# Seven-product matmuls one block earlier, sums kept in PSUM, and two units of work moved up

## The chip, the cores and the metric

The kernel runs on one core of one Trainium2 chip. The metric is device time in microseconds (us), the median of several runs. The engines are TensorE (PE in the rows; PEld is its weight load), VectorE (DVE), ScalarE (ACT), GpSimd (POOL) and SyncE (SP), which here issues most of the transfers. Each engine executes its own list of instructions in order and waits on semaphores for the others.

## The reference

Three parts follow one another: an attention with a memory term (B = 4, H = 8, S = 576, D = 64, so 2304 tokens), a first feed-forward layer (512 → 2048 → 512, softplus) and a second (512 → 2048 → 512, squared relu).

```python
local = softmax(causal(q @ k.T / 8)) @ v
mem = (phi(q) @ M_prev) / (phi(q) @ z_prev + 1e-06)
x = g * mem + (1 - g) * local          # 2304 tokens x 512
h = x @ w_in;  x = softplus(h) @ w_out    # layer 1
h = x @ w_in;  y = relu(h) ** 2 @ w_out   # layer 2, other weights
```

## The kernel before

Numbers are kept as a high and a low 16-bit part, so each product of two matrices is three matmuls on TensorE (high·high, high·low, low·high). The weights come as 64-bit data in 32 pieces per layer (512 KB each, buffer `wst`) and are converted on VectorE (L480 to L482, L490) and ScalarE (L489).

**Attention and layer 1.** Attention runs over 18 chunks of 128 tokens, in steps of a chunk and a group of heads: scores into `s_ps` (L342), the mask and the exponential, a transposing DMA (`PT`), the product with V into `pvt` (L399, L390). Layer 1 works on blocks of 256 tokens, `kb` = 0 to 8 there, and is cut into units: `h` (24 matmuls into `hps`, L502 to L504, then four ScalarE operations and two on VectorE that end in `g`, L506 to L513), `x` (96 matmuls into `xps`, L519 to L521), `xq` (a quarter of the contraction of block 0, into `xacc`, L564 to L566) and `w` (conversion of one piece). The units stand in a queue and are put between the attention steps as long as their added time stays under a limit; the limit for the queue ahead of a block leaves `LEAD_NS` (15000) of it for behind the last step. While layer 1's weights are still coming, block 0 is worked in quarters, and part of the units of block 1 is mixed in.

**Layer 2.** The weights W3 and W4 take memory that the attention used, and their conversion begins when it is free. The first 512 tokens are done plainly: `plain_h` (matmuls of 512 columns, L793 to L795, relu L797, square L798, a high part by a cast on VectorE, L801, and a low part, L802), then four `row_tile` (L988 to L990). The other seven blocks of 256 tokens (`kb` = 2 to 8 from here on) go by a scheme of seven products in place of eight: `x_parts`, `sums_w3` and `sums_w4` build sums of the inputs and of the weights (`XT`, `WS`, `WT`), `seven_h` does the first product of a block in two halves (q = 0, 1; each 7 × 24 matmuls of 128 columns), `parts` splits its result into `GA` and sums `GS`, and `seven_o` does the second product (two calls, together 168 matmuls of 256 columns). `plain_o` does the second product without the scheme (96 matmuls of 512 columns, L975 to L977); block 2 (`NPL` = 1) and block 8 use it. In both schemes each product has a PSUM bank of its own (pool `mm2`, eight banks), and VectorE adds it to the results (L886 to L895, L944).

A list scheduler orders each engine's instructions from the order of the code and priorities.

Of the kernel before, what the change touches and what calls it, by code (L numbers as in the profile page):

```python
# [8 lines left out]
F32 = mybir.dt.float32  # L9
# [9 lines left out]

LAG = 4  # L20
LEAD_NS = 15000.0
FR = 0.4
W1R = 1
B1Q = 3
# [19 lines left out]
NST = 3  # L44
PTB = 4
PB = 2
NPL = 1
W4A = (0, 2)
W4B = {1: (4,), 2: (6,)}
P16 = 2  # L50
ST2 = 4
DL = 2
# [3 lines left out]
def kernel(  # L56
# [101 lines left out]
    zc = att.tile([P, 2, B * H], F16, name="zc")  # L158

    def z_setup():  # L160
        zr = stage.tile([B * H, 2, D], F32, name="zr", bufs=1)
# [328 lines left out]
        dve.tensor_tensor(lo, u, hi, ALU.subtract)  # L490

    g_t = {}

    def unit_h(kb, fp):
# [15 lines left out]
        g = [w1p.tile([P, 2, NB], F16, name=f"g{t}_{fp}") for t in range(2)]  # L510
# [65 lines left out]

    load("k", 0)
    load("q", 0)
    load("k", 1, stage)
    load("v", 0)  # L580
    gates()
    z_setup()
# [113 lines left out]
    for kb in range(1, NBLK + 1):  # L696
        if kb == 1:
            lim = FR * sum(unit_time(u) for u in queue)
        else:
            lim = sum(unit_time(u) for u in queue) - LEAD_NS  # L700
        end = ready_step(kb) if kb < NBLK else s - 1
        if kb < NBLK:
            tot_c = sum(step_cost(i) for i in range(s, end + 1))
# [13 lines left out]
        if kb == 1:  # L717
            done = 4 - sum(u[0] == "xq" for u in queue)
            if done < 4:
                at = 0  # L720
                while done < B1Q:
                    done += queue[at][0] == "xq"
                    at += 1
                nh = 2 * done
                early = new[:nh] + [("x", kb, c, 0, 2 * nh) for c in range(NCC // 2)]
                out_q = queue[:at]
                for u in queue[at:]:
                    if u[0] != "w" and early:
                        out_q += early
                        early = []  # L730
                    out_q.append(u)
                    if u[0] == "w" and early:
                        out_q.append(early.pop(0))
                queue = out_q + early + [("close",)]
                if done < 4:
                    new = new[nh:]
                    xs = [("x", kb, c, 2 * nh, NFC) for c in range(NCC // 2)]
            else:
                queue.append(("close",))
# [13 lines left out]
    def w34_to(m):  # L753
        nonlocal nxt
        while nxt < m:
# [2 lines left out]
                pieces[nxt + ST2] = load_piece(nxt + ST2, (moe2_w_in, moe2_w_out), sp, st2)  # L758
            nxt += 1

    for n_, u in enumerate(queue):
        run_unit(u)
        w34_to(NPC * (n_ + 1) // nu)
    mm_cm.__exit__(None, None, None)
    pv_cm.__exit__(None, None, None)
    sps_cm.__exit__(None, None, None)
# [5 lines left out]
    mm2 = ctx.enter_context(tc.tile_pool(name="mm2", bufs=8, space=PSUM, reuse_waits="tile"))  # L772
    u2 = S_R / S_X2
    SO = 1.0 / (S_R * S_R)
    HF = NFC // 2
# [5 lines left out]


    def plain_h(j):
        x = x_t[0]
        new_g(j)
        for h in range(2):
            for i in range(2):
                f = h * HF + j + i
                ps = mm2.tile([P, 512], F32, tag="mm2", name="h2ps")
                for c in range(NCC):  # L790
                    wh, wl = (w[:, c, f * P:(f + 1) * P] for w in W3)
                    xh, xl = (x[:, t * NCC + c] for t in range(2))
                    pe.matmul(ps, wh, xh, start=(c == 0), stop=False)  # L793
                    pe.matmul(ps, wh, xl, start=False, stop=False)
                    pe.matmul(ps, wl, xh, start=False, stop=(c == NCC - 1))  # L795
                r = bp.tile([P, 512], F32, name="r2", bufs=3)
                act.activation(r, ps, AF.Relu, scale=u2)  # L797
                act.activation(r, r, AF.Square)  # L798
                hi, lo = (g[:, h, :, i * 256:(i + 1) * 256] for g in gg[j])
                r = r.rearrange("p (a t) -> p a t", a=2)  # L800
                dve.tensor_copy(hi, r)  # L801
                dve.tensor_tensor(lo, r, hi, ALU.subtract)  # L802


# [63 lines left out]
    def seven_h(kb, q):  # L868
        X = XT[kb % 2]

        def prod(w, x):
            ps = mm2.tile([P, 512], F32, tag="mm2", name="h2ps")
            for i in range(4):
                o = ps[:, i * P:(i + 1) * P]
                for k in range(2):
                    wh, wl = w3_at(w, k, 4 * q + i)
                    xh, xl = (y[:, x, k * P:(k + 1) * P] for y in X)
                    pe.matmul(o, wh, xh, start=(k == 0), stop=False)  # L878
                    pe.matmul(o, wh, xl, start=False, stop=False)  # L879
                    pe.matmul(o, wl, xh, start=False, stop=(k == 1))  # L880
            return ps.rearrange("p (j t) -> p j t", j=4)
# [12 lines left out]
        dve.tensor_tensor(r11, prod(1, 1), r11, ALU.add)  # L894
        dve.tensor_tensor(r12, prod(5, 2), r12, ALU.add)  # L895
        act.activation(r[0], r[0], AF.Relu, scale=u2)
        act.activation(r[0], r[0], AF.Square)

# [24 lines left out]
            sp.dma_start(out=out[p0:p0 + k_, :].rearrange("p (a c) -> p a c", a=2), in_=o[r0:r0 + k_])  # L923

    OB = {}


    PR = {1: (0, 0), 2: (1, 1), 4: (2, 5), 6: (3, 6), 7: (4, 4), 3: (5, 2), 5: (6, 3)}

    def seven_o(kb, which):  # L930
        def prod(n):
            gi, wi = PR[n]
            ps = mm2.tile([P, 512], F32, tag="mm2", name="ops")[:, :256]
            for j in range(HF):
                g = GA[kb, j // 4][:, :, gi] if gi < 3 else GS[kb, j // 4][:, :, gi - 3]
                gh, gl = g[:, 0, j % 4], g[:, 1, j % 4]
                wh, wl = w4_at(wi, j)
                pe.matmul(ps, gh, wh, start=(j == 0), stop=False)  # L938
                pe.matmul(ps, gh, wl, start=False, stop=False)  # L939
                pe.matmul(ps, gl, wh, start=False, stop=(j == HF - 1))  # L940
            return ps

        def add(o, ps, y):
            dve.scalar_tensor_tensor(o, ps, SO, y, ALU.mult, ALU.add)  # L944

        if which == 0:
            OB[kb] = TS[:, :, NB:]
        o = OB[kb]
        o11, o12, o21, o22 = (o[:, i] for i in range(4))
        if which == 0:  # L950
            act.activation(o12, prod(6), AF.Copy, scale=SO)
            add(o21, prod(7), o12)
            p5 = prod(5)
            add(o22, p5, o21)
            add(o12, p5, o12)
            add(o12, prod(3), o12)
            return
        p1 = prod(1)
        act.activation(o11, p1, AF.Copy, scale=SO)
        add(o[:, 1:], p1.rearrange("p (a c) -> p a c", a=1).to_broadcast([P, 3, 256]), o[:, 1:])  # L960
        add(o11, prod(2), o11)
# [35 lines left out]
    for j in range(0, HF, 2):  # L997
        plain_h(j)
        w34_to(NPC + 2 * j + 4)
    st2_cm.__exit__(None, None, None)  # L1000
    sp2 = ctx.enter_context(tc.tile_pool(name="sums", bufs=1, reuse_waits="tile"))
    WS = [sp2.tile([P, 4, 2, DFF // 2], t, name=f"WS{i}") for i, t in enumerate((F16, BF16))]
# [24 lines left out]
    for kb in range(K0, NBLK):  # L1027
        plain = kb < K0 + NPL or kb == NBLK - 1
        if K0 < kb < NBLK - 1:
            x_parts(kb + 1)  # L1030
        seven_h(kb, 0)
        if K0 < kb <= K0 + NPL:
            plain_o(kb - 1)
        elif kb > K0:
# [38 lines left out]
```

## Time and profile before

| | us |
|---|---|
| median of 3 runs | 943.59 (941.1 to 945.34) |
| profiled execution, its own time | 943.42 |
| its span | 941.6 |
| TensorE busy | 880.2 (93%) |
| VectorE busy | 728.3 (77%) |
| ScalarE busy | 613.6 (65%) |

The span runs from the first to the last recorded work of that execution; 1.8 us lie around it. Busy is time with an instruction in work on the engine. A busy TensorE isn't TensorE at its peak: its granted clock stands beside it in the rows. "X <- Y" among waits means that the first was ready to go but for the second.

### The profile page before, as it was taken

How to read it: one execution, taken by the hardware profiler on the slowest of the kernel's cores; microseconds unless marked ns; L12 is line 12 of the kernel's file. 1: busy time of each engine (PE TensorE's matmuls, PEld its weight loads, DVE VectorE, ACT ScalarE, POOL GpSimd, SP SyncE). 2: the span in 40 equal slices, each digit the busy share in tenths (PEclk: the TensorE clock that was granted, in tenths of full speed). 3: DMA queues.
4: the chain of work that ended last, by engine and by line, in shares of the span. 5: the costliest groups of instructions: out<-in, count | busy, mean ns of one | idle time of the engine just before them, and what ended most of it. 6: DMA issues, size and time to landing. Idle time of an engine off the chain costs nothing.

```text
span 941.6 us, 24682 instructions
## 1 busy us (share of the span) xinstructions
PE 880.2 (93%) x10385; PEld 730.7 (78%) x10394; DVE 728.3 (77%) x1474; ACT 613.6 (65%) x1160; POOL 2.2 (0%) x10
## 2 busy tenths in 40 slices
PE   5757999889999898999999999999999999999997
PEld 3346888679878897899988887444776999999983
DVE  6798999878757676667856699999997998767640
ACT  7977688679769695867958375663266656444530
POOL 0000000000000000000000000000000000000000
PEclk9879899899999999999999999999999999999999
DMA  9999998799876978658845666500000000000001
GB/s 234 205 217 203 223 206 177 133 150 150 130 131 117 144 134 127 116 101 131 136 86 75 171 199 182 178 22 23 24 2 24 2 24 1 25 24 2 24 13 34
DMA packets 285023, 101.24 MB, mean 108 GB/s; under 512 B 248048, under 2 KB 284400, under 8 KB 284912
## 3 DMA queue, kind: packets, MB, share of 16 engines
q1 hardware_dynamic: 284672, 99.65, 53.3%
q8 instruction: 81, 1.33, 0.6%
q14 instruction: 30, 0.25, 0.1%
q10 hardware_dynamic: 240, 0.02, 0.0%
HBM read 48.78 MB, written 4.72 MB: 57 GB/s over the span
## 4 chain that ended last, share of the span: by engine, by line
PE 52%; DVE 22%; ACT 10%; DMA 10%; issue 5%; SPq 0%; ACTq 0%; DVEq 0%
PE h2ps L878 4%; PE h2ps L879 4%; PE h2ps L880 4%; PE hps L503 4%; PE hps L502 4%; DMA rawq<-in_q_dram 4%; PE hps L504 4%; DMA PT<-p 3%; PE ops L940 3%; PE ops L938 3%; PE ops L939 3%; DVE wcv L481 3%; PE s_ps L342 3%; PE xps L520 3%; PE xps L519 3%
## 5 line engine op out<-in xcount | busy, mean ns | idle before, releaser
L502 PE MATMUL hps<-x,W 128*128 128x256 f16 x576 | 157.5, 275 | 3.8 <-DVE spa L509 1.8
L503 PE MATMUL hps<-x,W 128*128 128x256 f16 x576 | 158.1, 275 | 0.5 <-ACT x L545 0.4
L504 PE MATMUL hps<-x,W 128*128 128x256 f16 x576 | 157.8, 275 | 0.0
L520 PE MATMUL xps<-g,W 128*128 128x256 f16 x512 | 138.8, 273 | 2.4 <-DVE g L513 2.4
L519 PE MATMUL xps<-g,W 128*128 128x256 f16 x512 | 137.8, 273 | 3.3 <-ACT g L512 3.3
L521 PE MATMUL xps<-g,W 128*128 128x256 f16 x512 | 138.8, 273 | 0.0
L351 ACT ACTIVATE Pt<-Pt,cs 128x128 f32<-128x128 f32 (+4 forms) x144 | 84.6, 588 | 45.1 <-DVE cs L347 45.0
L342 PE MATMUL s_ps<-KT,qT 128*128 128x128 f16 (+2 forms) x992 | 75.4, 219 | 22.1 <-DVE cs L347 20.8
L375 DVE TENSOR_TENSOR p<-Pt,p 128x512 f16<-128x512 f32 (+2 forms) x100 | 66.5, 665 | 30.0 <-ACT p L374 29.8
L342 PEld LDWEIGHTS <-qT 128*128 128x128 f16 (+1 forms) x992 | 56.2, 103 | 40.3 <-issue 32.6
L347 DVE CUSTOM_DVE_ANT_0 Pt<-s_ps,mask 128x128 f32<-128x128 f32 (+3 forms) x128 | 61.8, 483 | 19.5 <-PE s_ps L342 19.2
L374 ACT ACTIVATE p<-Pt 128x512 f16<-128x512 f32 (+2 forms) x100 | 60.5, 605 | 15.0 <-DMA PT<-p 14.1
L503 PEld LDWEIGHTS <-W 128*128 128x128 f16 x576 | 56.8, 99 | 9.6 <-issue 3.4
L502 PEld LDWEIGHTS <-W 128*128 128x128 f16 x576 | 56.9, 99 | 7.7 <-DVE spa L509 1.1
L504 PEld LDWEIGHTS <-W 128*128 128x128 bf16 x576 | 56.8, 99 | 7.2 <-issue 0.8
L399 PE MATMUL pvt<-V,PT 128*128 128x64 f16 (+1 forms) x1392 | 58.8, 196 | 1.3 <-DMA PT<-p 1.3
L513 DVE TENSOR_TENSOR g<-spa,g 128x512 f16<-128x512 f32 x72 | 49.4, 685 | 11.2 <-ACT g L512 11.0
L509 DVE SCALAR_TENSOR_TENSOR spa<-hps,spa 128x512 f32<-128x512 f32 x72 | 49.4, 686 | 9.5 <-ACT spa L508 9.2
L519 PEld LDWEIGHTS <-W 128*128 128x128 f16 x512 | 50.0, 98 | 8.7 <-issue 3.3
L521 PEld LDWEIGHTS <-W 128*128 128x128 bf16 x512 | 50.1, 98 | 8.1 <-issue 2.7
L399 PEld LDWEIGHTS <-PT 128*128 128x128 f16 (+1 forms) x1392 | 51.2, 103 | 6.1 <-issue 2.1
L520 PEld LDWEIGHTS <-W 128*128 128x128 f16 x512 | 50.1, 98 | 5.2
(248 smaller groups left out, 2564.8 us busy)
## 6 DMA issues: line engine op xcount, KB each, us to landing
wst<-in_moe_w_in_dram SPq DMA_DIRECT2D x32, 512.0 KB, 4.7
wst<-in_moe_w_out_dram SPq DMA_DIRECT2D x32, 512.0 KB, 4.6
rawk<-in_k_dram SPq DMA_DIRECT2D x16, 256.0 KB, 4.2
rawq<-in_q_dram SPq DMA_DIRECT2D x16, 256.0 KB, 4.3
rawv<-in_v_dram SPq DMA_DIRECT2D x16, 256.0 KB, 3.4
out_dram<-T SPq DMA_DIRECT2D x12, 256.0 KB, 2.4
PT<-p SPq DMA_TRANSPOSE x100, 3.5
mraw<-in_M_prev_dram SPq DMA_DIRECT2D x8, 128.0 KB, 4.5
```

The source lines that it names most:

```text
L342: pe.matmul(o[x * n:(x + 1) * n], qT[g][:, t * H + h, x * n:(x + 1) * n], KT[kb][:, h, a - j * P:e - j * P], start=(t == 0), stop=(t == 1),)
L347: dve.tensor_tensor_reduce(out=pw, in0=view, in1=mw, scale=-0.125, scalar=3.0e38, op0=ALU.add, op1=ALU.min, accum_out=cs[:, 0, h:h + 1],)
L351: act.activation(pf, pf, AF.Exp, bias=cs[:, 0, h:h + 1], scale=-1.0, accum_out=cs[:, 1, h:h + 1],)
L374: act.activation(v16[:, :, 0], p, AF.Copy)
L375: p_lo.append(dve.tensor_tensor(v16[:, :, 1], p, v16[:, :, 0], ALU.subtract).ins.name)
L399: m = pe.matmul(o[r], t[:, o0 + i + y, r], V[kb][:, z, h, :], start=(i == 0 and y + z == 0), stop=(i == nb - 1 and y > 0),)
L502: pe.matmul(o, wh, x[:, c], start=(c == 0), stop=False)
L503: pe.matmul(o, wh, x[:, NCC + c], start=False, stop=False)
L504: pe.matmul(o, wl, x[:, c], start=False, stop=(c == NCC - 1))
L519: pe.matmul(ps, wh, gh, start=(f == f0), stop=False)
L520: pe.matmul(ps, wh, gl, start=False, stop=False)
L521: pe.matmul(ps, wl, gh, start=False, stop=(f == f1 - 1))
```

## The change

1. `NPL` becomes 0: block 2's second product too is done by `seven_o`; its `parts` build all sums, and the sums of W4 are made one step earlier (`W4B`).
2. In `seven_h` and `seven_o` one bank now takes four products (a), one two (c), one a single one (b). On the way a ScalarE copy takes partial results out between two products of the bank. Adds on VectorE per half of `seven_h` go from seven to three, per block of `seven_o` from six to three.
3. The last two `h` units of block 1 stand in the queue ahead of the last `xq`.
4. The limit ahead of the last block leaves 30000 in place of 15000.
5. The first two of the 16 products of `plain_h` are done into the two banks of `s_ps`, ahead of the last block's `x` units; `mm2` has six banks until `plain_h` ends, then a pool of eight follows.
6. `plain_h`'s high part is a ScalarE copy.
7. `seven_h(2, 0)` stands ahead of the last `row_tile`; the small tile `zr` and the second load of k use other buffers.

```diff
-NPL = 1
+NPL = 0
-W4B = {1: (4,), 2: (6,)}
+W4B = {0: (4,), 1: (6,)}
...
-            lim = sum(unit_time(u) for u in queue) - LEAD_NS
+            lim = sum(unit_time(u) for u in queue) - (LEAD_LAST if kb == NBLK - 1 else LEAD_NS)
...
+                at = queue.index(("xq", 0, 3))
+                queue[at:at] = new[nh:]
                 if done < 4:
-                    new = new[nh:]
+                    new = []
...
+    def h2_mm(ps, f):
+        x = x_t[0]
+        for c in range(NCC):
+            wh, wl = (w[:, c, f * P:(f + 1) * P] for w in W3)
+            xh, xl = (x[:, t * NCC + c] for t in range(2))
+            pe.matmul(ps, wh, xh, start=(c == 0), stop=False)
+            pe.matmul(ps, wh, xl, start=False, stop=False)
+            pe.matmul(ps, wl, xh, start=False, stop=(c == NCC - 1))
+
     for n_, u in enumerate(queue):
+        if n_ == nu - NCC // 2:
+            for f in range(2):
+                h2_mm(s_ps[:, f], f)
         run_unit(u)
...
-                dve.tensor_copy(hi, r)
+                act.activation(hi, r, AF.Copy)
                 dve.tensor_tensor(lo, r, hi, ALU.subtract)
...
-        act.activation(r11, prod(0, 0), AF.Copy)
-        dve.tensor_tensor(r12, prod(3, 4), r11, ALU.add)
-        dve.tensor_tensor(r22, prod(4, 5), r12, ALU.add)
-        dve.tensor_tensor(r21, prod(2, 6), r22, ALU.add)
-        p5 = prod(6, 3)
-        dve.tensor_tensor(r22, p5, r22, ALU.add)
-        dve.tensor_tensor(r12, p5, r12, ALU.add)
-        act.activation(r[1], r[1], AF.Relu, scale=u2)
+        (a, a4), (b, b4), (c, c4) = bank(), bank(), bank()
+        prod(a, 0, 0, True, True)
+        act.activation(r11, a4, AF.Copy)
+        prod(c, 6, 3, True, True)
+        prod(a, 3, 4, False, True)
+        act.activation(r12, a4, AF.Copy)
+        prod(b, 1, 1, True, True)
+        dve.tensor_tensor(r11, b4, r11, ALU.add)
+        prod(a, 4, 5, False, True)
+        act.activation(r22, a4, AF.Copy)
+        dve.tensor_tensor(r22, c4, r22, ALU.add)
+        prod(a, 2, 6, False, True)
+        act.activation(r21, a4, AF.Relu, scale=u2)
+        act.activation(r22, r22, AF.Relu, scale=u2)
         act.activation(r[1], r[1], AF.Square)
-        dve.tensor_tensor(r11, prod(1, 1), r11, ALU.add)
-        dve.tensor_tensor(r12, prod(5, 2), r12, ALU.add)
+        prod(c, 5, 2, False, True)
+        dve.tensor_tensor(r12, c4, r12, ALU.add)
...
         if which == 0:
             OB[kb] = TS[:, :, NB:]
+            AC[kb] = bank(), bank()
...
+            prod(a, 1, True)
+            copy(o11, a)
+            prod(c, 5, True)
+            prod(a, 6, False)
+            copy(o12, a)
+            b = bank()
+            prod(b, 2, True)
+            add(o11, b)
+            prod(a, 7, False)
+            copy(o22, a)
+            add(o22, c)
+            return
+        prod(c, 3, False)
+        add(o12, c)
         store(2 * kb, o[:, :2])
-        add(o21, prod(4), o21)
+        prod(a, 4, False)
+        copy(o21, a)
         store(2 * kb + 1, o[:, 2:])
...
-    for m in range(XB // P):
+    for m in range(XB // P - 1):
         row_tile(0, m, XB // 2)
+    seven_h(K0, 0)
+    row_tile(0, XB // P - 1, XB // 2)
```

How instructions stand on the engines, at three places. Names carry numbers that differ between the two programs; W_70 and W_71 are layer 1's second weights there, and lines are moved by one to thirty-five.

The first is TensorE's list in the weights' stretch, before: between attention matmuls (`pvt`, `s_ps`) stand those of the last `xq` (`xacc`), and the 48 matmuls of the last two `h` units of block 1 come some hundred matmuls further on.

```order
L390 LDWEIGHTS phiT
L390 MATMUL pvt<-Mt,phiT 128x64
L390 LDWEIGHTS phiT
L390 MATMUL pvt<-Mt,phiT 128x64
L564 LDWEIGHTS W_70
L564 MATMUL xacc_982<-g_6_2588,W_70 128x256
L565 LDWEIGHTS W_70
L565 MATMUL xacc_982<-g_6_2589,W_70 128x256
L342 LDWEIGHTS qT
L342 MATMUL s_ps<-KT,qT 128x128
```

The same place after the change, some rows ahead of the first `xacc` of the last `xq`:

```order
L303 MATMUL nps<-zc,phiT 128x1
L504 LDWEIGHTS W_68
L504 MATMUL hps<-x_61,W_68 128x256
L505 LDWEIGHTS W_68
L505 MATMUL hps<-x_61,W_68 128x256
L506 LDWEIGHTS W_69
L506 MATMUL hps<-x_61,W_69 128x256
```

The `h` unit's matmuls (`hps`) now come ahead of that `xacc`, and none are left behind it until block 2's.

The second place is the end of layer 1 on TensorE, where the last `h` unit of the last block ends; before:

```order
L504 LDWEIGHTS W_69
L504 MATMUL hps<-x_2724,W_69 128x256
L519 LDWEIGHTS W_70
L519 MATMUL xps<-g_0_9166,W_70 128x256
L520 LDWEIGHTS W_70
L520 MATMUL xps<-g_0_9167,W_70 128x256
L521 LDWEIGHTS W_71
L521 MATMUL xps<-g_0_9166,W_71 128x256
```

And after:

```order
L506 LDWEIGHTS W_69
L506 MATMUL hps<-x_2917,W_69 128x256
L772 LDWEIGHTS W_8815
L772 MATMUL s_ps<-x_61,W_8815 128x512
L773 LDWEIGHTS W_8815
L773 MATMUL s_ps<-x_61,W_8815 128x512
L774 LDWEIGHTS W_8816
L774 MATMUL s_ps<-x_61,W_8816 128x512
```

The `x` units' matmuls (`xps`) followed directly; now 24 matmuls of layer 2 into `s_ps`, of 512 columns, stand between.

The third is ScalarE's list at the second half of `seven_h` of block 2 (`r_...` are its results, `W_...` those of the next half or block in memory of W3); before:

```order
L885 ACTIVATE r_10469<-h2ps 128x512
L849 ACTIVATE XT_10159<-x_2722 128x256
L885 ACTIVATE W_9015<-h2ps 128x512
L822 ACTIVATE WT_10156<-T 128x2x512 x2
L892 ACTIVATE r_10470<-r_10470 128x1024
L893 ACTIVATE r_10470<-r_10470 128x1024
L892 ACTIVATE W_9016<-W_9016 128x2x512
L901 ACTIVATE GA<-r_10470 128x1024
L893 ACTIVATE W_9016<-W_9016 128x2x512
L896 ACTIVATE r_10469<-r_10469 128x1024
```

And after, where L905, L908, L912 and L915 take results out of one bank:

```order
L905 ACTIVATE r_10653<-h2ps 128x512
L864 ACTIVATE XT_10161<-x_2915 128x256
L908 ACTIVATE r_10653<-h2ps 128x512
L837 ACTIVATE WT_10158<-T 128x2x512
L912 ACTIVATE r_10654<-h2ps 128x512
L925 ACTIVATE GS<-W_8815 128x1024
L915 ACTIVATE r_10654<-h2ps 128x512
L925 ACTIVATE GS<-W_8816 128x1024
L916 ACTIVATE r_10654<-r_10654 128x512
L917 ACTIVATE r_10654<-r_10654 128x1024
```

One operation on `h2ps` per half has become four, each with other work between. On TensorE the third copy's product and its follower in that bank stand so; behind L895 of one product (weights `WS`) the next begins (weights `W`), with nothing in between:

```order
L894 LDWEIGHTS WS_10156
L894 MATMUL h2ps<-XT_10162,WS_10156 128x128
L895 LDWEIGHTS WS_10157
L895 MATMUL h2ps<-XT_10161,WS_10157 128x128
L893 LDWEIGHTS W_8815
L893 MATMUL h2ps<-XT_10161,W_8815 128x128
L894 LDWEIGHTS W_8815
L894 MATMUL h2ps<-XT_10162,W_8815 128x128
```

It is the only such place without other matmuls between two products of one bank.

## Rows read from the trace of the kernel before

**Rows 1.** The page: busy time of each engine (PE alone); granted clock in 40 slices.
```profile
PE 880.2 (93%) x10385; PEld 730.7 (78%) x10394; DVE 728.3 (77%) x1474; ACT 613.6 (65%) x1160; POOL 2.2 (0%) x10
...
PEclk9879899899999999999999999999999999999999
```

**Rows 2.** Busy time by stretch: start:end, length, engines, granted clock, DMA share, GB/s.
```profile
0.00:100.00 100.00, 67.95 (x658) 47.36 (x659) 81.12 (x221) 80.33 (x189) 2.24 (x10) 0.86 1.03 216
100.00:200.00 100.00, 88.23 (x1071) 78.11 (x1067) 89.92 (x201) 76.77 (x160) 0.00 (x0) 0.96 0.94 182
200.00:540.00 340.00, 331.38 (x4492) 294.88 (x4491) 233.22 (x528) 254.15 (x533) 0.00 (x0) 1.00 0.73 124
540.00:640.00 100.00, 98.10 (x660) 64.33 (x659) 99.05 (x186) 61.78 (x107) 0.00 (x0) 1.00 0.46 140
640.00:740.00 100.00, 97.91 (x1074) 70.22 (x1079) 91.80 (x137) 48.73 (x61) 0.00 (x0) 1.00 0.05 17
740.00:860.00 120.00, 120.00 (x1594) 113.45 (x1592) 100.25 (x158) 65.45 (x82) 0.00 (x0) 1.00 0.05 15
```

**Rows 3.** Busy time in shorter stretches, columns as above.
```profile
160.00:180.00 20.00, 16.23 (x181) 13.58 (x180) 18.33 (x41) 13.77 (x30) 0.00 (x0) 0.86 0.87 149
174.00:180.00 6.00, 5.18 (x47) 4.09 (x48) 6.00 (x13) 4.19 (x9) 0.00 (x0) 0.52 0.51 68
180.00:200.00 20.00, 15.99 (x213) 13.86 (x211) 14.42 (x34) 15.32 (x32) 0.00 (x0) 0.93 0.88 152
198.00:200.00 2.00, 2.00 (x11) 1.43 (x10) 1.52 (x4) 2.00 (x5) 0.00 (x0) 0.53 1.02 192
680.00:700.00 20.00, 18.23 (x327) 18.05 (x325) 19.89 (x32) 11.06 (x15) 0.00 (x0) 1.00 0.01 2
```

**Rows 4.** Waits of PE from 160 to 202 us: total, times, longest.
```profile
PE xps L519 <- ACT g L512: 2.5, 1, 2.5
PE xacc L564 <- ACT W L489: 2.2, 1, 2.2
```

**Rows 5.** Line L795, every third matmul of plain_h: ns, first and last start.
```profile
L795 PE MATMUL h2ps<-x,W x64: 379/379/379, 587.8 to 628.5; 128*128 128x512 f16 x64
```

**Rows 6.** Timeline of PE: 33 matmuls of 256 columns, then 40 of 128.
```profile
564.20 0.27 PE L519 MATMUL xps<-g,W 128*128 128x256 f16 x1
...
567.80 0.27 PE L519 MATMUL xps<-g,W 128*128 128x256 f16 x1
...
745.01 0.22 PE L878 MATMUL h2ps<-XT,W 128*128 128x128 f16 x1
...
747.25 0.22 PE L879 MATMUL h2ps<-XT,WS 128*128 128x128 f16 x1
```

**Rows 7.** Timeline of DVE: first conversion of W3, sixth sum of W4.
```profile
533.35 0.43 DVE L480 TENSOR_SCALAR wcv<-wst 128x512 int32<-128x512 int32 x1 [5.82 <-DMA wst<-in_moe_w_in_dram]
...
705.00 1.21 DVE L823 TENSOR_TENSOR WT<-T,WT 128x1024 bf16<-128x1024 f32 x1
```

**Rows 8.** Timeline of ACT: the last copy ahead of the last store.
```profile
936.82 0.60 ACT L978 ACTIVATE T<-ops 128x512 f32<-128x512 f32 x1 [9.12 <-PE ops L977]
```

**Rows 9.** Waits of PE from 540 to 600 us.
```profile
PE xps L520 <- DVE g L513: 1.4, 1, 1.4
PE xps L519 <- ACT g L512: 0.5, 1, 0.5
```

**Rows 10.** Waits of PE from 640 to 720 us.
```profile
PE h2ps L878 <- ACT W L897: 1.8, 1, 1.8
```

**Rows 11.** Four lines: ns least, median, most; the last with its mean.
```profile
L886 DVE TENSOR_TENSOR W<-h2ps,W x7: 679/683/684, 673.7 to 882.2; 128x512 f32<-128x512 f32 x7
...
L885 ACT ACTIVATE W<-h2ps x7: 575/597/597, 671.7 to 880.3; 128x512 f32<-128x512 f32 x7
...
L801 DVE CAST gg<-r x16: 416/420/421, 593.0 to 632.2; 128x512 f16<-128x512 f32 x16
...
L901 ACT ACTIVATE GS<-r 128x1024 f16<-128x1024 f32 x8 | 8.4, 1050 | 8.8 <-DVE r L915 8.5
```

More of the change, by code (lines that the diff above doesn't have):

```diff
@@ L21 @@
 LEAD_NS = 15000.0
+LEAD_LAST = 30000.0
 FR = 0.4
@@ L160, in z_setup @@
     def z_setup():
-        zr = stage.tile([B * H, 2, D], F32, name="zr", bufs=1)
+        zr = att.tile([P, H, D], F32, tag="xf", name="zr")[:B * H, :2]
         z16 = stage.tile([B * H, 2, 2, D], F16, name="z16", bufs=1)
@@ L492 @@
     g_t = {}
+    hcount = [0]
     def unit_h(kb, fp):
@@ L509, in unit_h @@
         dve.scalar_tensor_tensor(a, ps, 0.0, a, ALU.max, ALU.add)
-        g = [w1p.tile([P, 2, NB], F16, name=f"g{t}_{fp}") for t in range(2)]
+        slot = hcount[0] % (NFC // 2)
+        hcount[0] += 1
+        g = [w1p.tile([P, 2, NB], F16, name=f"g{t}_{slot}") for t in range(2)]
         g_t[kb, fp] = g
@@ L578 @@
     load("q", 0)
-    load("k", 1, stage)
+    load("k", 1)
     load("v", 0)
@@ L765 @@
     pv_cm.__exit__(None, None, None)
-    sps_cm.__exit__(None, None, None)
     w1_cm.__exit__(None, None, None)
@@ L771 @@
     bp = bp_cm.__enter__()
-    mm2 = ctx.enter_context(tc.tile_pool(name="mm2", bufs=8, space=PSUM, reuse_waits="tile"))
+    mm2_cm = tc.tile_pool(name="mm2", bufs=6, space=PSUM, reuse_waits="tile")
+    mm2 = mm2_cm.__enter__()
     u2 = S_R / S_X2
@@ L783, in plain_h @@
     def plain_h(j):
-        x = x_t[0]
         new_g(j)
@@ L788, in plain_h @@
                 f = h * HF + j + i
[L789 to L795, printed above, removed]
+                if f < 2:
+                    ps = s_ps[:, f]
+                else:
+                    ps = mm2.tile([P, 512], F32, tag="mm2", name="h2ps")
+                    h2_mm(ps, f)
                 r = bp.tile([P, 512], F32, name="r2", bufs=3)
@@ L869, in seven_h, with prod @@
         X = XT[kb % 2]
-        def prod(w, x):
-            ps = mm2.tile([P, 512], F32, tag="mm2", name="h2ps")
+        def prod(ps, w, x, first, last):
             for i in range(4):
@@ L877, in prod, with bank @@
                     xh, xl = (y[:, x, k * P:(k + 1) * P] for y in X)
[L878 to L881, printed above, removed]
+                    s = first and i == 0 and k == 0
+                    pe.matmul(o, wh, xh, start=s, stop=False, skip_group_check=True)
+                    pe.matmul(o, wh, xl, start=False, stop=False, skip_group_check=True)
+                    pe.matmul(o, wl, xh, start=False, stop=last and i == 3 and k == 1, skip_group_check=True)
+        def bank():
+            ps = mm2.tile([P, 512], F32, tag="mm2", name="h2ps")
+            return ps, ps.rearrange("p (j t) -> p j t", j=4)
         r = RB[2 * q:2 * q + 2]
         r11, r12, r21, r22 = r[0][:, 0], r[0][:, 1], r[1][:, 0], r[1][:, 1]
-        act.activation(r11, prod(0, 0), AF.Copy)
-        dve.tensor_tensor(r12, prod(3, 4), r11, ALU.add)
-        dve.tensor_tensor(r22, prod(4, 5), r12, ALU.add)
-        dve.tensor_tensor(r21, prod(2, 6), r22, ALU.add)
-        p5 = prod(6, 3)
-        dve.tensor_tensor(r22, p5, r22, ALU.add)
-        dve.tensor_tensor(r12, p5, r12, ALU.add)
-        act.activation(r[1], r[1], AF.Relu, scale=u2)
+        (a, a4), (b, b4), (c, c4) = bank(), bank(), bank()
[12 more added lines that the diff above has]
+        act.activation(r22, r22, AF.Relu, scale=u2)
         act.activation(r[1], r[1], AF.Square)
-        dve.tensor_tensor(r11, prod(1, 1), r11, ALU.add)
-        dve.tensor_tensor(r12, prod(5, 2), r12, ALU.add)
+        prod(c, 5, 2, False, True)
+        dve.tensor_tensor(r12, c4, r12, ALU.add)
         act.activation(r[0], r[0], AF.Relu, scale=u2)
@@ L925, with prod @@
     OB = {}
+    AC = {}
     PR = {1: (0, 0), 2: (1, 1), 4: (2, 5), 6: (3, 6), 7: (4, 4), 3: (5, 2), 5: (6, 3)}
     def seven_o(kb, which):
-        def prod(n):
+        def prod(ps, n, first):
             gi, wi = PR[n]
-            ps = mm2.tile([P, 512], F32, tag="mm2", name="ops")[:, :256]
             for j in range(HF):
@@ L937, in prod, with bank, copy, add @@
                 wh, wl = w4_at(wi, j)
[L938 to L944, printed above, removed]
+                pe.matmul(ps, gh, wh, start=(first and j == 0), stop=False, skip_group_check=True)
+                pe.matmul(ps, gh, wl, start=False, stop=False, skip_group_check=True)
+                pe.matmul(ps, gl, wh, start=False, stop=(j == HF - 1), skip_group_check=True)
+        def bank():
+            return mm2.tile([P, 512], F32, tag="mm2", name="ops")[:, :256]
+        def copy(o, ps):
+            act.activation(o, ps, AF.Copy, scale=SO)
+        def add(o, ps):
+            dve.scalar_tensor_tensor(o, ps, SO, o, ALU.mult, ALU.add)
         if which == 0:
             OB[kb] = TS[:, :, NB:]
+            AC[kb] = bank(), bank()
+        a, c = AC[kb]
         o = OB[kb]
@@ L950, in seven_o @@
         if which == 0:
[L951 to L956, printed above, removed]
+            prod(a, 1, True)
[9 more added lines that the diff above has]
+            add(o22, c)
             return
[L958 to L961, printed above, removed]
+        prod(c, 3, False)
+        add(o12, c)
         store(2 * kb, o[:, :2])
-        add(o21, prod(4), o21)
+        prod(a, 4, False)
+        copy(o21, a)
         store(2 * kb + 1, o[:, 2:])
@@ L999 @@
         w34_to(NPC + 2 * j + 4)
+    mm2_cm.__exit__(None, None, None)
+    sps_cm.__exit__(None, None, None)
+    mm2 = ctx.enter_context(tc.tile_pool(name="mm3", bufs=8, space=PSUM, reuse_waits="tile"))
     st2_cm.__exit__(None, None, None)
@@ L1030 @@
             x_parts(kb + 1)
-        seven_h(kb, 0)
+        if kb > K0:
+            seven_h(kb, 0)
         if K0 < kb <= K0 + NPL:
```

## Prediction

> **What bounds the kernel now.** I read the page's first two parts, then busy time by stretch, then what TensorE waited for in each stretch. The reader sees in [rows 1] that TensorE is busy 880.2 of 941.6 us and that its granted clock is at nine tenths or more from the ninth slice on. By stretch [rows 2]: TensorE is idle 32.0 us in the first 100 us, where the DMA engines are full (share 1.03), 11.8 us in the next 100, 8.6 in the 340 us up to 540, and then 1.9, 2.1 and 0.0. So from 200 us on, time falls mainly where matmul time falls, and only waits that the edits touch can be added. VectorE is the second limit: 99.05 of 100 us in 540 to 640, 91.8 in the next 100. ScalarE has room everywhere (61.8, 48.7, and 65.5 of 120).
>
> Inside the second 100 us there is more to gain than idle time. From 174 to 180 the granted clock is 0.52, the 1.2 GHz level, and again 0.53 at 198 to 200 [rows 3]; the full level is 2.4 GHz. Both stretches follow waits of TensorE: 2.2 us for a converted weight ahead of xacc and 2.5 us for g ahead of xps [rows 4].
>
> **The change, part by part.**
>
> Second product of block 2: 96 matmuls of 512 columns go, 168 of 256 come. One of 512 takes (628.5 − 587.8)/189 = 0.2153 us, since the row [rows 5] is every third of 192. One of 256 takes (567.80 − 564.20)/33 = 0.109 us [rows 6]. So 20.7 us go and 18.3 come: **−2.4 us**, all on TensorE. What could take it back is that its sums of W4 and of the activations are now wanted a block, about 37 us, earlier. VectorE works without a gap from the first conversion of W3 at 533.35 us to the sixth sum of W4, which ends at 706.2 [rows 7]. Those 172.9 us hold operations whose durations add up to 188.8 us, so one follows another at 0.916 of its duration. After the change, with the new adds in and the sixteen casts and the adds of seven_h out, the same count gives 174 us to the last sum of W4, 164 us to the activation sums GS of the block's first half, and 182 to those of the second. The first conversion waits for a transfer that waits for the end of the attention (its memory is used again), so it comes at 526 to 533 us; the two GS are then ready at 690 to 697 and 708 to 715. Counted back from the last copy at 936.82 [rows 8] with these pitches and 0.056 for 128 columns (2.24 us for 40 [rows 6]), TensorE comes to them with 238 and 221 us of matmuls left, that is at about 692 and 709 if it ends 7 us earlier. It is even within a few microseconds: I take 0, with bounds 0 and +5.
>
> The waits around the end of layer 1: 24 matmuls of 512 columns (24 × 0.2153 = 5.2 us) now stand between the last h unit and the x units that waited 1.4 + 0.5 us for its g [rows 9]. Their weights are converted and their data are there, since the two pieces of W3 that they take are converted first, by 540 us, and the layer's first block is long done. 5.2 us cover 1.9: **−1.9 us**.
>
> The wait of 1.8 us in 640 to 720 for a square of seven_h(2,0) [rows 10], with VectorE busy 19.89 of 20 us there [rows 3]: four of seven VectorE adds of each half leave (8 × 0.683 = 5.5 us [rows 11]), but the fuller split of block 2 brings four of about that length and larger pieces. I take **−1.2 us**, bounds −1.8 and 0.
>
> The early units: two h units of block 1, 48 matmuls or 5.2 us at full clock, move ahead of the last xq, where TensorE waited 2.2 and then ran at half speed. The 5.2 busy us from 174 to 180 lost half to the clock, 2.6, and the 2.0 at 198 to 200 lost 1.0; with the 4.7 us of the two waits up to 8 us could come back. But VectorE is busy 18.33 of 20 us in 160 to 180 [rows 3], and each h unit gives it two operations and ScalarE four, which delays the attention's own chain. I take a third: **−3.0 us**, bounds 0 and −8. The pieces of W are converted in the same order, and the move of one DMA of k on SP's queue is in a stretch where the DMA engines are full either way: 0.
>
> The copies moved to ScalarE in plain_h: 16 × 0.42 leave VectorE [rows 11] and 16 of about 0.6 (0.597 for a copy of the same size [rows 11]) come to ScalarE, which has 38 us free in that 100. Cost 0 there; without that room it would be 10 us.
>
> Accumulation in PSUM: in each half of seven_h four products share one bank, and a ScalarE copy (0.597 us) stands between two of them; seven_o has three such places per pair. ScalarE gains about 1.35 us a half and 0.75 a seven_o, 3.5 us per block of 37, and VectorE loses 7.3 (8 × 0.683, and 1.8 of seven_o's adds). Before, every product had its own bank and TensorE is busy 120.00 of the 120 us from 740 on [rows 2]. After, the order shows what stands between two products to one bank: of some 80 places one has nothing (seven_h(2,1), the last rows of the order shown), which costs about 0.6 + 0.3 = 0.9 us; the others have 1.6 us of other matmuls or more, half of them over 2.8. A copy fits into 1.6 us unless an operation of 1.05 us [rows 11] stands ahead of it on ScalarE, which then makes it late by about 0.1. I take **+1.3 us**, bounds +0.9 and +10: the last if a fourth of the places, the tightest 20, lose 0.5 each.
>
> The Trainium skill speaks against this edit: "Perfetto Trace Analysis", section "Optimizing Tensor Performance", wants independent groups of matmuls to rotate through PSUM banks so that one's evacuation runs under the next one's matmuls. The trace of before agrees with what that buys (the same 120.00 of 120 us). By the rule the change would end at the upper bound, +10, and the time at 945.6.
>
> Attention before the last block ends 37 matmuls, 4.0 us, earlier. As much cover is gone from a stretch with 8.6 us of idle time in 340: **+0.7**, bounds 0 and +4. seven_h(2,0) before the last row_tile only fills: 0. The second product of the last block keeps its form and has about 10 us of matmuls ahead of its last input, so the end of the span (last matmul, a ScalarE copy, a store) stays.
>
> Sum: −2.4 − 1.9 − 1.2 − 3.0 + 1.3 + 0.7 = −6.5. The profiled execution took 943.42 us (span 941.6 and 1.8 around it), 0.2 under the median of 943.59, so 943.42 − 6.5 = **936.9 us**.
>
> **The rivals.**
>
> A. *The early part gives nothing.* VectorE or the transfers set the pace up to 200 us, and the h units only change places with other waits. For it: VectorE at 18.33 of 20, the DMA share. Against it: TensorE is idle 7.8 us in the 40 us from 160 on [rows 3]. Without the −3.0 the time is 939.9.
>
> B. *The sums are late.* VectorE ends its chain 5 us after TensorE wants it, and the −2.4 and −1.9 turn into waits for GS or WT at 690 to 715. For it: VectorE at 99%. Against it: 6.7 us of casts and 5.5 of adds leave this stretch. Then 936.9 + 5 = 941.9.
>
> C. *Slower: the shared bank.* ScalarE executes in order; behind an operation that waits for VectorE the copy is late, and TensorE, in order as well, stands at the next product of the bank. There are about 80 places; from 0.1 us at each on average (8 us instead of 1.3) the other gains are gone. At 0.2 us each (16 instead of 1.3) the time is 951.6; with the 10 of the bound it is 945.6. For it: three times as many handovers between ScalarE and TensorE. Against it: 1.6 us of cover, and ScalarE at two thirds.
>
> D. *The whole bound of the early part comes back.* The clock stays at full level from 172 to 202: −8 for −3, 931.9.
>
> By the Trainium skill's "Perfetto Trace Analysis", section "Matmul Optimizations", matmuls that run back to back keep TensorE's speed up, which agrees with the clock of 0.52 after the wait and would speak for D.
>
> **How the numbers follow.** The forecast (934 to 938.8) has 0.38, A 0.20, B 0.18, C 0.11 and D 0.13. A measurement of this kernel tells about 0.5% (4.7 us) from no change: under 938.9 is faster, over 948.3 slower. Faster: forecast and D, 0.51, and a third of A, where the other terms come out a little better: 0.58. Same: the rest of A, B, and a third of C: 0.35. Slower: the rest of C, 0.07. The range takes in D below, with 2 us for its own error, and leaves out the far part of C above: 930 to 946.
>
> **What would show it.** Seven-product matmuls at 256 columns in place of 512 around 700 us, and no row of a wait there over 1 us; else B. No wait of xps for g after the last h unit, 1.9 us less. At 165 to 205 us fewer idle microseconds and a granted clock over 0.9; else A. From 740 on TensorE's busy time of 120 in 120; waits for a ScalarE copy at h2ps or ops there, more than 5 us in all, would be C and would make the prediction wrong, as would attention steps waiting longer for VectorE in 500 to 540.

## The result and the profile after

The changed kernel takes 934.74 us (median of 4 runs, 933.26 to 936.56); beside it the kernel before took 944.47. The ratio is 0.9908 with a 95% interval of 0.9885 to 0.9931, which is 8.7 us (the medians are 9.7 apart). A second time, with a set of the runs below, the ratio was 0.9922 (0.9891 to 0.9952). The profiled execution took 934.81 us, its span is 932.9.

The page of the changed kernel, busy time and granted clock:

```profile
PE 877.5 (94%) x10466; PEld 737.9 (79%) x10466; DVE 692.4 (74%) x1395; ACT 644.9 (69%) x1232; POOL 2.2 (0%) x10
...
PEclk9978999999999899999999999999999999999999
```

VectorE lost 35.9 us of work and ScalarE gained 31.3; TensorE's busy time, in which a matmul at half clock counts double (128 columns start 0.11 us apart behind 687.3 us, 0.055 ahead of it), fell 2.7. Busy time by stretch, columns as in [rows 2]:

```profile
0.00:100.00 100.00, 66.69 (x652) 46.19 (x653) 80.72 (x220) 79.60 (x189) 2.23 (x10) 0.86 1.08 217
100.00:200.00 100.00, 93.62 (x1163) 84.54 (x1162) 94.71 (x210) 80.00 (x165) 0.00 (x0) 1.00 0.95 177
200.00:540.00 340.00, 331.82 (x4466) 294.58 (x4465) 238.17 (x537) 253.02 (x534) 0.00 (x0) 0.99 0.73 131
540.00:640.00 100.00, 100.00 (x638) 62.27 (x637) 98.38 (x171) 69.68 (x120) 0.00 (x0) 1.00 0.40 122
640.00:740.00 100.00, 97.01 (x1203) 82.30 (x1201) 87.21 (x129) 60.72 (x83) 0.00 (x0) 0.98 0.04 15
740.00:860.00 120.00, 120.00 (x1612) 113.61 (x1611) 71.20 (x103) 71.57 (x104) 0.00 (x0) 1.00 0.05 15
```

And in shorter stretches; the third and the fifth are those at half clock behind two new waits:

```profile
160.00:180.00 20.00, 19.46 (x240) 17.43 (x238) 17.86 (x40) 14.95 (x31) 0.00 (x0) 1.00 0.85 144
180.00:200.00 20.00, 17.85 (x258) 16.23 (x256) 18.34 (x42) 15.77 (x35) 0.00 (x0) 1.00 0.83 135
315.20:322.04 6.84, 5.78 (x44) 4.35 (x45) 3.84 (x11) 2.63 (x7) 0.00 (x0) 0.50 0.71 125
680.00:700.00 20.00, 17.32 (x231) 16.30 (x229) 19.51 (x30) 14.47 (x19) 0.00 (x0) 0.91 0.01 2
687.27:690.68 3.41, 3.41 (x29) 3.15 (x29) 3.41 (x5) 3.15 (x6) 0.00 (x0) 0.50 0.00 0
```

The reader sees where the time came from. The granted clock of a stretch is a mean over its whole length, so 0.96 over 100 us is 4.0 us lost. In the second 100 us TensorE is idle 6.4 us where it was 11.8, and its clock is 1.00 where it was 0.96: 9.4 us less. In 540 to 640 the idle 1.9 us are gone. The reader also sees what was given back: behind a wait for a transfer TensorE runs at the 1.2 GHz level from 315.2 to 322.0, which costs half of 5.8 busy us (2.9), and in 640 to 740 idle time rose from 2.1 to 3.0 with 3.4 us at that level (1.7). With 1.3 us more idle time in the first 100, 0.4 less in 200 to 540, 0.4 less in the tail and 2.4 us fewer matmuls, that makes −9.4 + 1.3 + 2.9 − 0.4 − 1.9 + 0.9 + 1.7 − 0.4 − 2.4 = −7.7 of the span's −8.7; the remaining 1.0 is not placed.

TensorE's waits of the changed kernel, from 300 to 330 us and from 600 to 740 us; in 540 to 600 there is none:

```profile
PE hps L504 <- DMA x<-xn: 2.6, 1, 2.6
...
PE h2ps L893 <- DVE r L913: 2.0, 1, 2.0
PE h2ps L893 <- ACT r L912: 0.7, 1, 0.7
PE h2ps L893 <- ACT W L905: 0.3, 1, 0.3
```

The third is the place without cover that the prediction priced at 0.9. The second is new: in the second half of seven_h of block 2, the last product goes into bank c only when VectorE has read what stands in it (L913). Against [rows 10] the wait has changed its cause and not gone. The prediction's own sign for rival B, a wait over 1 us around there, has come.

### The profile page after: what moved, and what is told of

It reads as the page before. It is cut to its first block, busy times and chain, and to the rows that moved or that the text cites. A ratio compares the mean times of both kernels' runs of the same rounds, so it can differ in the third digit from the quotient of the medians.

```text
span 932.9 us, 24770 instructions
## 1 busy us (share of the span) xinstructions
PE 877.5 (94%) x10466; PEld 737.9 (79%) x10466; DVE 692.4 (74%) x1395; ACT 644.9 (69%) x1232; POOL 2.2 (0%) x10
## 4 chain that ended last, share of the span: by engine, by line
PE 54%; DVE 21%; DMA 10%; ACT 10%; issue 4%; SPq 1%; DVEq 0%; ACTq 0%
PE h2ps L893 4%; PE h2ps L895 4%; PE h2ps L894 4%; PE ops L962 4%; PE ops L963 4%; PE ops L964 4%; DMA PT<-p 4%; PE hps L504 3%; PE hps L505 3%; PE hps L506 3%; PE xps L524 3%; PE xps L525 3%; PE s_ps L343 3%; PE xps L523 3%; DVE wcv L482 3%
## 5 line engine op out<-in xcount | busy, mean ns | idle before, releaser
L343 PE MATMUL s_ps<-KT,qT 128*128 128x128 f16 (+2 forms) x992 | 75.8, 219 | 19.8 <-DVE cs L348 19.5
L504 PEld LDWEIGHTS <-W 128*128 128x128 f16 x576 | 57.2, 99 | 11.1 <-DMA x<-xn 2.8
L505 PEld LDWEIGHTS <-W 128*128 128x128 f16 x576 | 57.1, 99 | 7.6 <-issue 0.9
L490 ACT ACTIVATE W<-wcv 128x512 f16<-128x512 f32 x56 | 35.1, 626 | 35.8 <-DVE wcv L483 35.6
L523 PEld LDWEIGHTS <-W 128*128 128x128 f16 x512 | 50.1, 98 | 5.5
```

The costliest lines, as they stand in the source:

```text
L343: pe.matmul(o[x * n:(x + 1) * n], qT[g][:, t * H + h, x * n:(x + 1) * n], KT[kb][:, h, a - j * P:e - j * P], start=(t == 0), stop=(t == 1),)
L523: pe.matmul(ps, wh, gh, start=(f == f0), stop=False)
```

## The experiments

All ratios are to the kernel before, run on the same chip, with a 95% interval. The runs were made in three groups on three chips, so they are compared by ratio; where an expectation names a time, it is set against the 944.47 above (942 is 0.997, 934 is 0.989).

**One part undone at a time.** The early units back behind the last `xq`:

```diff
...
-                at = queue.index(("xq", 0, 3))
-                queue[at:at] = new[nh:]
                 if done < 4:
-                    new = []
+                    new = new[nh:]
...
```

The buffers of g are taken as before the change too.

> The changed kernel with the last two h units of block 1 back behind the last xq, nothing else undone. Theory: the early units filled TensorE's waits at 172 and 198 us and kept its clock at the full level; the 9.5 us of idle and half-speed time that left 160 to 210 us come back, most of them to the end: about 942 us, and the granted clock shows a stretch near 0.5 between 165 and 205. Rival: the early part is set by the transfers and VectorE, and the gain lies elsewhere: 934 to 936 us.

Measured: 937.46 us, 0.9959 (0.9934 to 0.9985), 3.5 to 4.8 us behind the changed kernel's two ratios. Its stretches from 160 on (columns as before):

```profile
160.00:180.00 20.00, 16.54 (x187) 14.41 (x186) 16.72 (x37) 13.59 (x29) 0.00 (x0) 0.91 0.78 139
180.00:200.00 20.00, 16.49 (x218) 14.23 (x216) 15.63 (x36) 15.57 (x33) 0.00 (x0) 0.91 0.97 175
```

TensorE is idle 7.0 us at a clock of 0.91 (before the change 7.8 us, at 0.86 and 0.93), behind the two waits of [rows 4], from 160 to 202 us:

```profile
PE xps L520 <- ACT g L513: 2.7, 1, 2.7
...
PE xacc L565 <- ACT W L490: 1.7, 1, 1.7
```

The theory's mechanism is shown, and its 0.997 lies in the interval, the rival's 0.989 to 0.991 outside. Of its 9.5 us 3.5 to 4.8 reached the end.

Block 2's second product plain again (`NPL = 1`, `W4B = {1: (4,), 2: (6,)}`):

> The changed kernel with block 2's second product plain again (96 matmuls of 512 columns, the sums of W4 one step later). Theory: 2.4 us of matmuls come back, but the waits of 2.0 and 0.7 us around 685 us fall, since VectorE has less to do there: 935 to 937.5 us. Rival: the matmuls alone count, 937.1 or more. Other rival: the sums one block earlier cost more than the matmuls saved: under 934 us.

Measured: 930.56 us, 0.9877 (0.9840 to 0.9914). It isn't slower than the changed kernel, by the ratios 3 to 4 us faster, though the intervals overlap; that is the second rival's range (under 0.989). Its busy times in 640 to 740 and in 680 to 700, and TensorE's only wait in 600 to 740 us:

```profile
640.00:740.00 100.00, 99.21 (x1165) 77.37 (x1171) 80.84 (x120) 58.71 (x81) 0.00 (x0) 1.00 0.04 15
...
680.00:700.00 20.00, 19.84 (x227) 14.62 (x228) 8.61 (x14) 13.71 (x19) 0.00 (x0) 1.00 0.00 1
```

```profile
PE h2ps L893 <- ACT W L905: 0.4, 1, 0.4
```

Against the changed kernel's 97.01 and 3.4 us at half clock that is 2.2 us of idle time and 1.7 of clock less, for 2.4 us more matmuls: the scheme saves in this block no more than its waits cost. VectorE is busy 8.61 of 20 us around 690, where it was busy 19.51, and the wait for it is gone.

The two products of `plain_h` behind the `x` units again (the call of `h2_mm` stands in `plain_h` for them too):

> The changed kernel with the first two products of plain_h done behind the last x units instead of ahead of them. Theory: TensorE waits 1.4 to 1.9 us for g again between the last h and the first x unit: 936.5 us, a row of that wait near 560 us. Rival: the following stretch, where VectorE is at 98 of 100 us, gives the same end: 934.7 us.

Measured: 934.18 us, 0.9916 (0.9890 to 0.9942): no difference that can be told, and theory (0.992) and rival (0.990) both lie in the interval. The wait is back, at a third of its size (from 540 to 600 us):

```profile
PE xps L524 <- DVE g L517: 0.6, 2, 0.3
```

The lead ahead of the last block (`LEAD_LAST = 15000.0`):

> The changed kernel with a lead of 15000 ahead of the last block too, as before the change. Theory: denser attention cost 0.7 us, and nothing waits for the conversions that begin up to 4 us earlier: 934 us. Rival: VectorE's chain from the first conversion of W3 to the sums sets the waits at 685 us, and begins 4 us later: TensorE waits there 2 to 4 us more, 937 to 939 us.

Measured: 935.44 us, 0.9935 (0.9913 to 0.9957), 1.2 to 2.5 us behind, with intervals that overlap. It missed the theory's 934 (0.989). The time is the rival's (0.992 to 0.994), but not its cause: TensorE's waits from 600 to 740 us are 3.2 us in all, where the changed kernel has 3.0. No wait of TensorE between 480 and 600 us explains it either.

**One part done alone.** For these the changed kernel was run beside:

> The changed kernel itself on the chip of the runs beside it, so that they have it to stand against: 0.991 of the kernel before, as measured, with the same waits of 0.7 and 2.0 us near 685 us.

Measured: 932.59 us, 0.9922 (0.9891 to 0.9952), with waits near 685 us of 1.7 and 0.7 us. Two of its stretches:

```profile
100.00:200.00 100.00, 93.88 (x1107) 83.75 (x1106) 92.80 (x205) 79.32 (x162) 0.00 (x0) 0.96 0.92 178
...
640.00:740.00 100.00, 97.61 (x1215) 81.88 (x1213) 88.30 (x131) 61.00 (x83) 0.00 (x0) 1.00 0.04 15
```

So a single profile places the half clock badly: around 690 none followed the waits this time, and in the second 100 us, where the first profile has a full clock, it is 0.96, in part behind a wait of 3.0 us for a transfer (`PT`) at 160 us. That full clock is the rule all the same: of the eleven profiles with the early units only this one falls under 0.99 there, and the three without them have 0.96 to 0.97.

The kernel before with the early units alone:

```diff
...
+                at = queue.index(("xq", 0, 3))
+                queue[at:at] = new[nh:]
                 if done < 4:
-                    new = new[nh:]
+                    new = []
...
```

> The kernel before with nothing changed but the two h units ahead of the last xq (and the buffers of g by turn). Theory: the 12.5 us of idle and half-speed time between 160 and 210 fall to about 3, and 4 to 9 us of it reach the end: ratio to before 0.990 to 0.996. Rival: the early part only trades waits, or needs the other edits: 0.999 to 1.001.

Measured: 942.75 us, 1.0019 (0.9999 to 1.0039): nothing, where taking the same edit out cost 3.5 us or more. From 160 to 210 us the profile has 3.6 us of idle time and a full clock, much as the changed kernel; over the second 100 us it gains 10.0 us (5.8 idle at 1.00 against 11.8 at 0.96). The gain was lost later, in three places. The first is a wait for x, with half clock behind it:

```profile
PE hps L503 <- DMA x<-xn: 4.0, 1, 4.0
...
314.20:321.10 6.90, 4.64 (x39) 3.57 (x40) 4.10 (x10) 3.36 (x10) 0.00 (x0) 0.51 0.98 193
```

The clock costs 2.3 us there, and idle time in 200 to 540 is 10.4 us where it was 8.6. The early units bring this wait: every run that has them has it, with 2.6 to 4.0 us, but for the last one below, which changes the order ahead of it; the kernel before, the changed kernel without them and the kernel with the PSUM edit alone have none. What holds that transfer no run shows. The second place is at the windows (560 to 580 us), first before the change, then here:

```profile
560.00:580.00 20.00, 18.15 (x165) 15.97 (x164) 19.97 (x36) 13.40 (x23) 0.00 (x0) 1.00 0.55 165
...
560.00:580.00 20.00, 16.81 (x137) 13.83 (x135) 19.96 (x37) 13.08 (x23) 0.00 (x0) 0.92 0.54 170
```

The `x` units wait 3.2 us for g instead of 1.9 [rows 9], and the clock falls behind that (1.3 and 1.6 us):

```profile
PE xps L523 <- DVE g L516: 1.6, 3, 1.1
PE xps L522 <- ACT g L515: 1.6, 1, 1.6
```

The third shows in no wait and no idle time; it is found on the timeline of TensorE near 500 us, where the attention's last, half-size chunk is worked (matmuls of the form 128*64):

```profile
495.71 0.28 PE L504 MATMUL hps<-x,W 128*128 128x256 f16 x1
495.83 0.22 PE L342 MATMUL s_ps<-KT,qT 128*128 128x128 f16 x1
495.88 0.27 PE L505 MATMUL hps<-x,W 128*128 128x256 f16 x1
...
500.08 0.27 PE L505 MATMUL hps<-x,W 128*128 128x256 f16 x1
500.19 0.27 PE L503 MATMUL hps<-x,W 128*128 128x256 f16 x1
500.30 0.27 PE L504 MATMUL hps<-x,W 128*128 128x256 f16 x1
500.51 0.24 PE L342 MATMUL s_ps<-KT,qT 128*64 128x128 f16 x1
500.68 0.28 PE L505 MATMUL hps<-x,W 128*128 128x256 f16 x1
500.89 0.24 PE L342 MATMUL s_ps<-KT,qT 128*64 128x128 f16 x1
501.07 0.28 PE L503 MATMUL hps<-x,W 128*128 128x256 f16 x1
501.28 0.24 PE L342 MATMUL s_ps<-KT,qT 128*64 128x128 f16 x1
```

Three `hps` matmuls in a row start 0.11 us apart; behind them the next starts after 0.21, and from one `hps` to the next it is 0.39 us, where an `hps` and a full-size score matmul take 0.109 + 0.056 = 0.165 [rows 6]. The first three rows are the same alternation with a full-size score matmul: 0.17 from `hps` to `hps`. So it is the change of form that costs, 0.22 us for each pair of changes, and TensorE counts as busy. In this kernel's list one `hps` or `xps` matmul stands alone between two score matmuls at 23 places, in the kernel before at 4, in the changed one at 3, with the lead of 15000 at 18. Some of these neighbours are full-size (all of them where there are 3 or 4), so the changes of form themselves, counted on the timelines behind 400 us, are the better measure: 80 here, 50 before, 46 in the changed kernel, 72 with the lead of 15000. Thirty more at 0.11 are 3.3 us. The three places together, some 10 us, take back what the early units gain.

The kernel before with nothing but the two functions that add up in PSUM:

> The kernel before with nothing changed but seven_h and seven_o adding up in PSUM. Theory: the copies fit between the products, VectorE loses 7 us a block that nothing waits for from 740 us on, and the wait of 1.8 us near 688 shrinks: ratio 0.997 to 1.000, no wait at h2ps or ops from 740 on. Rival (one bank for four products makes TensorE wait for the copies): 0.1 to 0.2 us at each of some 80 places, ratio 1.008 to 1.016.

Measured: 942.53 us, 1.0008 (0.9987 to 1.0029). From 740 on no wait, and TensorE is full:

```profile
740.00:860.00 120.00, 120.00 (x1618) 113.72 (x1617) 74.23 (x107) 73.90 (x107) 0.00 (x0) 1.00 0.05 15
```

The rival's 1.008 is excluded. No gain can be told either (the theory's upper end, 1.000, lies in the interval): the wait of [rows 10] grew from 1.8 to 2.9 us, for a square of the same half (600 to 740 us):

```profile
PE h2ps L878 <- ACT W L906: 2.9, 1, 2.9
```

A bank of its own for the product that waits for L913:

```diff
-        prod(c, 5, 2, False, True)
+        if kb == K0 and q == 1:
+            dve.tensor_tensor(r12, c4, r12, ALU.add)
+            c, c4 = bank()
+            prod(c, 5, 2, True, True)
+        else:
+            prod(c, 5, 2, False, True)
```

> The changed kernel, where in the second half of seven_h of block 2 the last product (5, 2) gets a bank of its own and VectorE one add more, so that it does not wait until VectorE has read bank c. Theory: the wait of 2.0 us for that add and the stretch at half clock behind it (1.5 us) go: 3 us less than the changed kernel. Rival: VectorE is full there, and TensorE waits for the next thing that VectorE is late with: the changed kernel's time within 1 us, or more, by the added add.

Measured: 934.41 us, 0.9930 (0.9906 to 0.9954), no better than the changed kernel beside it. The wait moved to the sums (600 to 740 us):

```profile
PE ops L967 <- ACT GS L930: 4.9, 1, 4.9
```

That is the rival's picture: freeing the bank does not help, and TensorE waits for the next thing. VectorE is busy 20.00 of the 20 us from 680 on; whether its load is the cause, the cast below tests.

**The lead and the changes of form.** The kernel before with the early units and the lead of 30000:

> The kernel before with two edits: the early h units, and a lead of 30000 ahead of the last block. Theory: the early units gain some 6 us by 400 us, and it was the order at the end of the attention that took them back when they stood alone (single matmuls of the half-size last chunk between single hps matmuls, 23 places against 4); with the other lead there are 3 such places: 0.993 to 0.996 of before. Rival: the gain needs the other edits (the buffers of z and k), and this stays at 0.999 to 1.002.

Measured: 935.12 us, 0.9931 (0.9914 to 0.9948). Against the early units alone the lead is worth 8 us, and most of the whole change's gain is in these two edits; the other buffers for z and k, the rival, are not needed for it. From 560 to 580 us, where the early units alone had 16.81 at 0.92:

```profile
560.00:580.00 20.00, 18.30 (x165) 15.95 (x164) 19.86 (x37) 10.05 (x18) 0.00 (x0) 1.00 0.58 184
```

1.5 us of idle time and 1.6 of clock are back, and with 32 changes of form fewer (48 against 80) some 3.5 us; that is 6.6 of the 8. The wait for x stays (3.8 us).

The changed kernel with a lead of 20000:

> The changed kernel with a lead of 20000 ahead of the last block. Its list has 3 single hps matmuls between scores, as with 30000, where a lead of 15000 has 18. Theory: it is these places, each some 0.1 us twice, that cost 2 to 3 us with 15000, so 20000 gives the time of the changed kernel: 0.990 to 0.993 of before. Rival: the lead itself (the earlier start of the conversions) is what counts: a third of the way only, 0.993 to 0.995.

Measured: 932.98 us, 0.9912 (0.9894 to 0.9930): the changed kernel's time, with 42 changes of form. It goes with the count of changes and not with the lead. The intervals of this and of the lead of 15000 (0.9913 to 0.9957) overlap, so this alone would not settle it.

**VectorE's chain.** The cast of `plain_h` on VectorE again:

> The changed kernel with plain_h's high part cast on VectorE again (16 x 0.42 us). Theory: VectorE's chain from the conversion of W3 to the sums is what TensorE waits for at 685 us, so the chain ends about 6 us later and the waits in 640 to 710 us grow by 3 to 6 us: 0.994 to 0.998 of before. Rival: the wait there is one of order, not of load: within 1 us of the changed kernel.

Measured: 936.07 us, 0.9947 (0.9926 to 0.9967), 2.3 to 3.7 us behind the changed kernel. The waits from 600 to 740 us:

```profile
PE ops L962 <- ACT GS L925: 3.1, 1, 3.1
PE ops L963 <- DVE WT L838: 0.7, 1, 0.7
PE h2ps L893 <- ACT r L912: 0.7, 1, 0.7
PE ops L964 <- DVE GA L926: 0.2, 1, 0.2
```

4.7 us, where the changed kernel had 3.0, now for the sums themselves; the growth is under the 3 to 6 us expected. With more work on VectorE and 8.5 us less on ScalarE (636.4 busy in place of 644.9) the waits grew, and with less on VectorE (the plain product) they went: VectorE's chain is what TensorE waits for there.

**A better version, tried.** Plain product and a lead of 26000 ahead of block 4:

> The changed kernel with block 2's second product plain again, and a lead of 26000 ahead of block 4 of layer 1, where TensorE waited 2.6 us for a transfer of x and then ran at half clock. Theory: both gains add up: 1.3 us or more for the plain product, 3 to 5 us for the wait: 0.983 to 0.986 of before. Rival: the denser attention ahead of block 4 waits for VectorE instead: 0.987 to 0.990.

Measured: 940.64 us, 0.9997 (0.9983 to 1.0011): the wait for x is gone, and 11 us are lost against the plain product alone. From 240 to 300 us TensorE is busy 53.74 us at 0.95, where with the plain product alone it is busy 58.38 at 1.00; the waits there:

```profile
PE s_ps L343 <- DVE cs L348: 3.2, 4, 2.0
PE nps L303 <- DMA phiT<-phin: 2.1, 1, 2.1
```

Its largest wait is the rival's, for VectorE, at more than the rival's price; the second is for a transfer. The stretch accounts for some 7.6 of the 11 us, the rest is not placed. The fastest kernel measured is the one with the plain product and the other leads (0.9877).

## Why the prediction was right, and which terms were not

The time of 934.74 lies 2.2 under the 936.9 forecast, and so does the ratio's 8.7 against the 6.5 added up. The terms fared unevenly.

**Early units, −3.0.** Right in mechanism and too small: the 12 us of idle and half-clock time from 160 to 210 fell to 3, in the second profile to 4; the wait for x near 314 us, which the early units bring, and the half clock behind it took a part back, and 3.5 to 4.8 us reach the end. Rival A, that this part gives nothing, does not hold for the whole change, but it describes the edit alone, by causes that it didn't name: the wait for x, a longer wait for g and more changes of form. Rival D's full clock came, and not its whole gain at the end.

**Denser attention, +0.7.** The step that failed in sign. I priced the lead as lost cover and each part as if it stood alone. What the lead did was to keep the last chunk's half-size matmuls from being mixed singly with full-size ones, which the early units would do (50 changes of form become 80, and 48 with the lead), and to shorten the wait for g. With the early units it is worth 8 us in the kernel before, and 1.2 to 2.5 in the changed one, where the two products into `s_ps` cover the wait already. No run has the lead without the early units.

**Products into `s_ps`, −1.9.** The wait went as forecast, but leaving the edit out showed no measurable loss: 0.6 us of wait came back, not 1.9.

**Block 2's second product, −2.4, and the wait of 1.8, −1.2.** The matmuls were saved and given back. "It is even within a few microseconds: I take 0" held for the sums that it counted: the two GS were ready at 690.7 and 709.0 us, and TensorE didn't wait for them. What it left out is an add that frees bank c, for which VectorE came 2.0 us late. Idle time in 640 to 740 rose by 0.9 and the clock took 1.7 more, in the second profile 0.3 and nothing, so that the two terms together give +0.2 to −2.1 instead of −3.6; undone, the kernel isn't slower. The cause is that of rival B, VectorE late: with the bank freed the wait moved to GS, with less on VectorE it went, with more it grew.

**Accumulation, +1.3.** About +1 ± 2 us when done alone; no wait at `h2ps` or `ops` from 740 on, so rival C is excluded. The one place without cover cost 0.7 of the 0.9 forecast. The rule of the Trainium skill ("Perfetto Trace Analysis", section "Optimizing Tensor Performance"), by which the change would end at 945.6, does not bind here: with the other matmuls that stand between two products of a bank, 1.6 us or more by the prediction's count, the copy of 0.6 us hides.

**The sum.** Undone one at a time, the lead and the early units gave 2.4 to 5.0 us more than forecast, and accumulation is within its error of the forecast; block 2 gave 1.5 to 3.8 less and the products into `s_ps` about 1 less. The casts moved to ScalarE, priced at 0, are worth 2.3 to 3.7 us when undone, since they take load off VectorE. These figures overlap, and the errors cancel in part: that the time came out closer than its terms is luck. Idle time in the first 100 us, where these kernels are the same, is 33.3 and 36.7 us in the two profiles of the changed kernel and 31.2 with the plain product, so one profile of each places no term closer than its ratio does.

## What to carry to other kernels

An edit that moves work forward pays only if every later handover follows: the same two units gave nothing alone and 6 us with another lead, so undo parts and also do them alone. Look at the pitch of instructions, not only at waits: a TensorE that is busy 20.00 of 20 us can be slow by the order of its matmuls. Where a second engine has no room (VectorE here, 19.5 of 20 us), saved matmuls turned into waits, and freeing the place that waited moved the wait on.

## What the runs showed of the hardware that was not expected

A change between matmuls of the form 128*128 and of the form 128*64 costs about 0.1 us each way (0.39 us for a pair that takes 0.165 in one form, and 0.17 with a full-size score matmul between), without idle time in the profile. The Trainium skill states the kind of it, in "TensorEngine Tiling (Array Packing)", section "Key Properties": a change of tiling mode drains TensorE. The trace agrees that the change costs time, and puts the price on it; that it is a drain no run here shows. Matmuls of the half form next to each other overlap: in the kernel with the early units alone, four score matmuls took 0.30 us where a single one is given 0.24, though full-size ones of 128 columns start 0.056 us apart.

```profile
502.06 0.30 PE L342 MATMUL s_ps<-KT,qT 128*64 128x128 f16 x4
```
